# Folding a block-diagonal feature map into projection weights: one product of 128 rows, or two of 64 rows into two PSUM banks

## The chip, the cores and the metric

The kernel runs on one core of a Trainium2 chip. The metric is the device time of one execution in microseconds. A core has a matrix engine (PE in the profile, with its weight loads shown apart as PEld), a vector engine (DVE), a scalar engine (ACT), a general engine (POOL) and queues that issue DMA transfers (SP). PE writes its products to PSUM, which has eight banks; DVE and ACT read them from there.

## The reference, cut to what matters

Two models of width 1024 with 32 heads of 32 run on their own inputs of 2048 rows, and their outputs are put side by side. The first (A) is an attention with a compressed memory. The second (B) is a linear attention whose queries and keys pass through a learned map, one 32x32 matrix for each head, before two softmaxes:

```python
qkv = (x @ wqkv).reshape(B, S, 3, H, Dh).transpose(2, 0, 3, 1, 4)
q, k, v = qkv[0], qkv[1], qkv[2]
pq = einsum("bhsd,hdf->bhsf", q, w_phi)
pk = einsum("bhsd,hdf->bhsf", k, w_phi)
phi_q = concatenate([softmax(pq), softmax(-pq)], -1)
phi_k = concatenate([softmax(pk), softmax(-pk)], -1)
kv = einsum("bhsf,bhsd->bhfd", phi_k, v);  z = einsum("bhsf->bhf", phi_k)
o = einsum("bhqf,bhfd->bhqd", phi_q, kv) / (einsum("bhqf,bhf->bhq", phi_q, z)[..., None] + 1e-6)
return o.transpose(0, 2, 1, 3).reshape(B, S, D) @ wo
```

As (x @ w) @ phi = x @ (w @ phi), the kernel multiplies the weights of q and k by the map once and never computes q and k themselves.

## The kernel before, in words

**Stages.** From the start to about 900 us the attention of model A runs, in 32 units (`units`): a unit is one segment of 512 rows and one group of four heads. `produce` computes the projections of a unit, `values` its values, `attend` its scores, softmax, products with the values, and memory. Model B's keys and values follow, then its queries and output, then A's output projection. Large products are made of f16 halves (three products for each fp32 one) and partly by a Strassen scheme of seven products for eight.

**The fold.** Model B's weights are prepared while A runs. `fold(n, ...)` is called once for each unit, from `attend(u)` for unit u + 1, between the memory part and the scores, and once at the start; 32 calls in all. Four calls make one `quad`: 128 feature columns at two places of the output and two halves of the 1024 input columns. A call loads a tile `st` [128, 512] of transposed weights: 128 rows are the features of one group of four heads, 512 columns are inputs of the model. `phib` [128, 8, 128] holds the map; for each group its 128x128 block is zero but for four 32x32 blocks on the diagonal, one for each head. For each of four chunks of 128 columns, `st`'s chunk is the stationary operand (loaded as weights of the array) and `phib`'s block is streamed, all in fp32, into one PSUM bank [128, 4, 128] (line 1006). DVE then reads the bank, scales it by the factor `si` and writes a quarter of the quad in SBUF (line 1009). When a quad is whole, POOL forms sums and differences of its quarters (line 458), ACT and POOL split them into f16 halves (lines 465 and 466), and DMAs put them into the scratch tensor `wf_d`. Model B reads these forms much later. A call also loads the next quad's piece and measures its size (`size`, lines 980 to 994).

**The order of the work.** No engine's order is written by hand. Every operation is entered with `op(engine, dur, fn, r=..., w=..., prio=...)`: the microseconds that the planner books for it, what it reads and writes, and a priority. `Graph.run` then plays a list scheduler over those durations: it takes the engine that can start first and, on it, the startable operation with the lowest priority number, and emits the instructions in that order. The order is fixed before the kernel runs; on the chip the engines wait for each other by semaphores. `attend(u)` has priority 2u + 1, `fold` for the next unit 2u, `produce(u + 1)` 2u + 2.

**PSUM.** `bank(kind, shape, line)` asks the planner for one of the eight banks, and it is given at the first operation that uses it and comes free after the last. Kinds have a minimum that is kept for them and a maximum:

```python
KEEP = {"proj": 1, "s": 1, "misc": 1, "pv": 1, "kv": 0}
MOST = {"proj": 3, "s": 3, "misc": 2, "pv": 1, "kv": 4}
```

The fold uses a bank of the kind `misc`, and so do the row maxima (line 793), the memory's products (820), the transposed keys and the memory's update (835, 840), the transposed output (933), and the small products for scales and bounds (370, 657, 678). An operation that needs a bank starts when one can be given to its kind. Operations with the same `line` name open their banks in the order in which they were entered.

Of the kernel before, what the change touches and what calls it, by code (L numbers as in the profile page):

```python
# [13 lines left out]
OP = mybir.AluOpType  # L14
# [52 lines left out]
class Graph:  # L67
# [35 lines left out]
    def op(self, eng, dur, fn, r=(), w=(), prio=0, lat=0.0, short=False, port=False, need=(), kb=256):  # L103
        o = Op()
        o.short, o.port = short, port or eng == "POOL"
        o.eng, o.dur, o.fn, o.prio, o.lat, o.kb = eng, dur, fn, (prio, len(self.ops)), lat, kb
        o.banks = []
        ends, starts = set(), set()
        for b in need:
            if b.prev[0] is not None:  # L110
                ends.update(b.prev[0].ops)
        for write, accs in ((0, r), (1, w)):
            for acc in accs:
                b, key = acc if isinstance(acc, tuple) else (acc, None)
                old, last, opened = b.prev
                if old is not None:
                    ends.update(old.ops)
                if not b.ops and last is not None:
                    starts.add(last.ops[0])
                if opened is not None:  # L120
                    starts.add(opened)
                for k in (list(b.writer) if key is None else [key, None]):
                    if k in b.writer:
                        ends.add(b.writer[k])
                if write:
                    for k in (list(b.readers) if key is None else [key, None]):
                        ends.update(b.readers.pop(k, ()))
                    if key is None:
                        b.writer.clear()
                    b.writer[key] = o  # L130
                else:
                    b.readers.setdefault(key, []).append(o)
                b.ops.append(o)
                if b.kind is not None and b not in o.banks:
                    o.banks.append(b)
                    b.left += 1
        ends.discard(o)
        o.deps = [(d, 0) for d in ends] + [(d, 1) for d in starts - ends if d is not o]
        self.ops.append(o)
        return o  # L140
# [99 lines left out]
SP, PE, ACT, DVE, POOL = "SP", "PE", "ACT", "DVE", "POOL"  # L240
# [3 lines left out]
def tile_kernel(ctx: ExitStack, tc: tile.TileContext, ax, aw, awv, awo, beta, bx, bwqk, bwv, bphi, bwo, out):  # L244
    nc = tc.nc
# [68 lines left out]
    for t in vfb:  # L314
# [3 lines left out]
    op = G.op  # L318
# [5 lines left out]
       w=[gates], prio=0.2, lat=2.0, kb=16)  # L324
# [14 lines left out]
    def bank(tag, shape, line=None):  # L339
        b = G.bank(tag, shape, F32, line or tag)  # L340
        psums.add(b)
        return b
# [246 lines left out]
    for t in stk:  # L589
        op(ACT, 2.0, lambda t=t: nc.scalar.activation(t()[96:104, 1], sel[96:104, :, None].to_broadcast([8, 4, 512]), AF.Copy),  # L590
           w=[(t, (1, 3))], prio=0.3)
# [146 lines left out]
    def attend(u):  # L738
# [108 lines left out]
        if u + 1 < NU:  # L847
            fold(u + 1, 2 * u + 0)
# [92 lines left out]
    phib = G.buf("a", [128, NG, 128], F32, "phib")  # L941
# [25 lines left out]
    def fold(n, prio, dep=()):  # L967


        m, i = divmod(n, 4)  # L970
        which, gp, q, hb = 1 - m // 4, m % 4, i % 2, i // 2
        g = gp + 4 * hb

        def load(m, i):
            st = G.buf("stage", [128, 512], F32, "st", 2)
            op(SP, 0.6, lambda: nc.sync.dma_start(st(), bwqk[1 - m // 4, m % 4 + 4 * (i // 2), :, 512 * (i % 2):512 * (i % 2) + 512]),
               r=dep, w=[st], prio=prio, lat=1.0)
            return st

        def size(m, i):  # L980
            if i == 0:
                sizes[m] = (G.buf("a", [128, 4], F32, "twf", 1), G.buf("a", [128, 2], F32, "sif", 2))
            tw, si = sizes[m]
            st = load(m, i)
            op(ACT, 0.55, lambda: nc.scalar.activation(st(), st(), AF.Abs, accum_out=tw()[:, i:i + 1]), w=[st, (tw, i)], prio=prio)
            if i % 2:
                h = i // 2
                op(DVE, 0.1, lambda: nc.vector.scalar_tensor_tensor(
                    tw()[:, h:h + 1], tw()[:, 2 * h:2 * h + 1], tw()[:, i:i + 1], phs[:, m % 4 + 4 * h:m % 4 + 4 * h + 1],
                    op0=OP.max, op1=OP.mult), r=[(phss, m % 4 + 4 * h)], w=[tw], prio=prio)  # L990
            if i == 3:
                scale((tw, lambda: tw()[:, 0:2]), 2, (si, None, si), prio, top=13)
                op(DVE, 0.06, lambda: nc.vector.tensor_copy(swf[:, 1 - m // 4, m % 4:m % 4 + 1], si()[:, 0:1]),
                   r=[si], w=[(swfs, (1 - m // 4, m % 4))], prio=prio)

        if n == 0:
            for j in range(4):
                size(0, j)
        si = sizes[m][1]
        if i == 0:  # L1000
            quads[m] = G.buf("a", [128, 4, 512], F32, "quad", 1)
        qd = quads[m]
        st = load(m, i)
        ps = bank("misc", [128, 4, 128], "fold")
        for c in range(4):
            op(PE, 0.22, lambda c=c: nc.tensor.matmul(ps()[:, c, :], st()[:, c * 128:(c + 1) * 128], phib()[:, g, :],
                                                      start=True, stop=True), r=[st, phib], w=[ps], prio=prio, need=[qd])
        k = 2 * q + hb
        op(DVE, 0.62, lambda: nc.vector.tensor_scalar(qd()[:, k], ps().rearrange("p c n -> p (c n)"), si()[:, 1:2], None, op0=OP.mult),
           r=[ps, si], w=[(qd, k)], prio=prio)  # L1010
        if m < 7:
            size(m + 1, i)
        if i == 3:
            quads["prio"] = prio + 3
            forms(WPLAN, lambda k: (qd, k, lambda: qd()[:, k]),
                  out_halves(which, ("fo", "oT"), lambda d: d.rearrange("p a c n -> p (a c) n")[:, :, 128 * gp:128 * gp + 128]),
                  None, prio + 3, POOL)
# [44 lines left out]
    for f in (lambda: bounds(0, [1], 2.5), lambda: bounds(1, [1], 2.5), lambda: bounds_v(0, [1], 2.5)):  # L1062
        f()
    fold(0, 1, late)
    for u in range(NU):
        k = u // 2
# [65 lines left out]
    def pairv(t):  # L1132

        return t().rearrange("p (h a g d) -> p h a g d", h=2, a=2, g=8)
# [77 lines left out]
    for p in range(NT // 2):  # L1212
# [17 lines left out]
        for i in range(2):  # L1230
            if p in VT:
                n = 2 * VT.index(p) + i
                for hb in range(2):
                    op(SP, 0.6, lambda n=n, hb=hb, t=vs[i]: nc.sync.dma_start(
                        t()[:, 1056 * hb:1056 * hb + 1056], v_d[n, :, 1056 * hb:1056 * hb + 1056]), r=[(vdb, (n, hb))],
                       w=[(vs[i], (a, hb)) for a in range(2)] + [(vs[i], 2)], prio=P - 0.5, lat=1.5, kb=256)
# [8 lines left out]
        for hb in range(2):  # L1245
            for j in range(2):
                kv = bank("kv", [128, 4, 66], "sums")
                for i in range(2):
                    pt = G.buf("b", [128, 4, 4, 128], F16, "pt", 3)

                    def flat(e=es[i, hb], j=j):
# [3 lines left out]
                       r=[es[i, hb]], w=[(pt, 0)], prio=P)  # L1255
                    sub, ns, d = ((DVE, nc.vector, 0.6) if i else (POOL, nc.gpsimd, 1.28))
                    op(sub, d, lambda pt=pt, flat=flat, ns=ns: ns.tensor_tensor(pt()[:, 1], flat(), pt()[:, 0], op=OP.subtract),
                       r=[es[i, hb], (pt, 0)], w=[(pt, 1)], prio=P, port=True)

                    def f(i=i, j=j, hb=hb, kv=kv, t=vs[i], pt=pt):  # L1260
                        for k in range(4):
                            for a, b in ((0, 0), (0, 1), (1, 0)):
                                n = 64 if b else 65
                                nc.tensor.matmul(kv()[:, k, 0:n], pt()[:, a, k, :], pairv(t)[:, hb, b, 4 * j + k, 0:n],
                                                 start=(i == 0 and k == 0 and a + b == 0), stop=(i == 1 and a == 1), skip_group_check=True)
# [3 lines left out]
                def add(o, i, s, p=p):  # L1269
# [7 lines left out]
                   r=[kv, (pstb, (p, 0))], w=[(kva[hb], j)], prio=P)  # L1277
# [6 lines left out]
    for q in range(4):  # L1284
        ps = bank("misc", [128, 512])
        for i in range(4):
            op(PE, 0.22, lambda i=i, q=q, ps=ps: nc.tensor.matmul(
                ps()[:, 128 * i:128 * i + 128], za()[:, 4 * q + i:4 * q + i + 1].to_broadcast([128, 128]), ident,
                start=True, stop=True), r=[(za, (q // 2, q % 2))], w=[ps], prio=P)
# [3 lines left out]
       r=[(bigs, 1)], w=[(oscs, 1)], prio=P - 5)  # L1293
    op(DVE, 0.12, lambda: nc.vector.reciprocal(osc2[:, 1, 1:2], osc2[:, 1, 0:1]), w=[(oscs, 1)], prio=P - 5)
    kls = [G.buf("stage", [128, 2, 8, 64], F16, "st", 2) for _ in range(2)]
    for hb in range(2):
        zr, zs, v = G.buf("b", [128, 8], F32, "zr", 2), G.buf("b", [128, 8, 2], F32, "zs", 2), slice(8 * hb, 8 * hb + 8)
        op(DVE, 0.1, lambda zr=zr, v=v: nc.vector.tensor_scalar(zr(), za()[:, v], 1e-12, None, op0=OP.max),
           r=[(za, (hb, 0)), (za, (hb, 1))], w=[zr], prio=P)
        op(DVE, 0.12, lambda zr=zr: nc.vector.reciprocal(zr(), zr()), w=[zr], prio=P)  # L1300
        op(DVE, 0.1, lambda zr=zr: nc.vector.tensor_scalar(zr(), zr(), osc2[:, 1, 1:2], 2.0, op0=OP.mult, op1=OP.mult),
           r=[(oscs, 1)], w=[zr], prio=P)
        op(DVE, 0.1, lambda zr=zr, zs=zs: nc.vector.tensor_tensor(
            zs(), zr()[:, :, None].to_broadcast([128, 8, 2]), bm2[:, None, :].to_broadcast([128, 8, 2]), op=OP.mult),
           r=[zr], w=[zs], prio=P)
# [4 lines left out]
           r=[kva[hb]], w=[(kls[hb], 0)], prio=P)  # L1310
        op(DVE, 0.62, lambda hb=hb, v=v: nc.vector.tensor_tensor(kls[hb]()[:, 1], kva[hb](), kls[hb]()[:, 0], op=OP.subtract),
           r=[kva[hb], (kls[hb], 0)], w=[(kls[hb], 1)], prio=P, port=True)
    op(DVE, 0.1, lambda: nc.vector.tensor_scalar(osc2[:, 0, 0:1], big[:, 0:1], 4.0, None, op0=OP.mult),
       r=[(bigs, 0)], w=[(oscs, 0)], prio=P)
# [4 lines left out]
       r=[(wscs, (1, 0)), (wscs, (1, 1)), (oscs, 1)], w=[wo2b], prio=P)  # L1319
# [15 lines left out]
    for n in range(2):  # L1335
        for q in range(2):
            op(SP, 0.6, lambda n=n, q=q: nc.sync.dma_start(bo[n][q](), bo_d[n, q]), r=[(bob, (n, q))],
               w=[(bo[n][q], (a, i)) for a in range(2) for i in range(4)], prio=P + 1, lat=1.0, kb=1024)
# [44 lines left out]
    for c in range(NT):  # L1383
# [15 lines left out]
        if c == 14:  # L1399
            for i, f in enumerate(SECOND):  # L1400
                wform[f] = G.buf("slot", [128, 2, 4, 512], F16, f"S{i}")
                op(SP, 0.6, lambda i=i, f=f: nc.sync.dma_start(wform[f](), wo_d[i]), r=[(wob, i)],
                   w=[(wform[f], (a, n)) for a in range(2) for n in range(4)], prio=P + 0.5, lat=1.0, kb=1024)
# [5 lines left out]
        for hb in range(2):  # L1409
            e, r = er[c % 2, hb]  # L1410
            dn = G.buf("b", [128, 16, 2], F32, "dn", 2)
            for a in range(2):
# [3 lines left out]
                   r=[zb, r], w=[(e, ("x", a))], prio=P)  # L1416
# [10 lines left out]
               r=[e, r], w=[e], prio=P)  # L1427
            def flat(e=e):
# [4 lines left out]
               r=[e], w=[(eh, (hb, 0))], prio=P)  # L1433
            op(DVE, 1.13, lambda eh=eh, hb=hb, flat=flat: nc.vector.tensor_tensor(
                eh()[:, hb, 1], flat(), eh()[:, hb, 0], op=OP.subtract), r=[e, (eh, (hb, 0))], w=[(eh, (hb, 1))], prio=P, port=True)
            for a in range(2):
                op(SP, 0.6, lambda a=a, eh=eh, hb=hb, pt=pt: nc.sync.dma_start_transpose(pt()[:, a], eh()[:, hb, a]),
                   r=[(eh, (hb, a))], w=[(pt, a)], prio=P, lat=2.0, kb=256)
            pn = bank("pv", [128, 4, 128])

            def f(pn=pn, pt=pt, hb=hb):
# [11 lines left out]
               r=[pn, (ot, (0, hb))], w=[(ot, (1, hb))], prio=P)  # L1453
# [6 lines left out]
    for c in range(NT // 2):  # L1460
        P += 1
        A0, A1 = (G.buf("b", [128, 2, 4, 128], F32, "e", 5) for _ in range(2))
        for t, k in ((A0, c), (A1, c + 8)):
            op(SP, 0.6, lambda t=t, k=k: nc.sync.dma_start(t().rearrange("p h g t -> p (h g) t"), oa_d[k]),
               r=[osc], w=[t], prio=P, lat=1.0, kb=512)
# [105 lines left out]
```

## Time and profile before

| | |
|---|---|
| median of 3 runs | 1761.08 us (1757.87 to 1761.38) |
| profiled execution | 1762.63 us, span 1760.8 us |
| PE busy | 1692.6 us, 96% |
| DVE busy | 1404.1 us, 80% |
| ACT busy | 1129.7 us, 64% |
| POOL busy | 968.4 us, 55% |
| fold's products (line 1006) | 256 records, first at 62.3 us, last at 843.6 us |
| fold's DVE reads (line 1009) | 32 of 744 ns |

The span is the time from the first to the last instruction of one profiled execution. A record of PE lasts from its start until its result is out, so records of products overlap, and the pace of PE is read from start to start. PEld is the loading of weights, which overlaps the products before it. In a group's row stand the line, engine, operation, tiles and shapes, the count, and then busy microseconds, mean nanoseconds of one, and the idle time of the engine just before, with what ended it. In a timeline's row stand the start in microseconds, the time to the end of the last of the merged instructions, and their count.

### The profile page before, as it was taken

What the parts mean: (1) busy time and instruction counts of PE and PEld (TensorE: products, weight loads), DVE (VectorE), ACT (ScalarE), POOL (GpSimd) and SP (SyncE); (2) the same over time, 40 slices, a digit from 0 to 9 for tenths busy, and PEclk for the clock granted to TensorE, in tenths of its full rate; (3) what the DMA queues carried; (4) which work ended last, traced back from release to release, by engine and by line L of the source; (5) the groups of instructions that cost most, each with busy time, mean ns of one, the idle gap of its engine ahead of it and who ended that gap; (6) DMA issues with size and microseconds to landing.
All of it is one profiled execution on the core that took longest, in us unless ns stands there. A gap on an engine that the chain in (4) does not pass through costs nothing.

```text
span 1760.8 us, 38488 instructions
## 1 busy us (share of the span) xinstructions
PE 1692.6 (96%) x14456; PEld 1013.5 (58%) x14456; DVE 1404.1 (80%) x3207; ACT 1129.7 (64%) x2063; POOL 968.4 (55%) x1301
## 2 busy tenths in 40 slices
PE   8999999999999999999989999999899999989999
PEld 5767666667776766766744444444444444444444
DVE  5989989899777888788875998996988777677541
ACT  6887886978776787777774656554665544444431
POOL 6445454555757577866773535553578989650000
PEclk8999999999999999999999999999999999999999
DMA  5546546475445444567456343346646666665311
GB/s 191 183 147 178 143 144 182 150 219 170 145 137 152 119 134 122 152 197 184 129 183 254 114 140 137 138 146 236 225 138 168 156 164 147 141 187 159 120 66 66
DMA packets 240842, 275.67 MB, mean 157 GB/s; under 512 B 137488, under 2 KB 190480, under 8 KB 231952
## 3 DMA queue, kind: packets, MB, share of 16 engines
q1 hardware_dynamic: 240656, 273.22, 51.0%
q8 instruction: 113, 1.85, 0.4%
q14 instruction: 73, 0.60, 0.1%
HBM read 145.44 MB, written 85.00 MB: 131 GB/s over the span
## 4 chain that ended last, share of the span: by engine, by line
PE 58%; DVE 19%; ACT 5%; POOL 3%; issue 2%; DMA 1%; SPq 0%; ACTq 0%; DVEq 0%
PE proj L359 19%; PE proj L549 9%; PE proj L1499 5%; PE misc L359 5%; PE s L865 3%; PE pv L901 3%; PE s L767 2%; PE s L1499 2%; DVE s L773 2%; PE s L549 2%; DVE mx L1110 2%; DVE S L388 2%; DVE r L1120 1%; POOL e L1414 1%; PE misc L1499 1%
## 5 line engine op out<-in xcount | busy, mean ns | idle before, releaser
L359 PE MATMUL proj<-S,S 128*128 128x128 f16 (+1 forms) x3072 | 504.0, 300 | 5.2 <-ACT S L386 3.3
L359 PEld LDWEIGHTS <-S 128*128 128x128 f16 x4608 | 331.8, 99 | 154.8 <-issue 10.7
L549 PE MATMUL proj<-S,S 128*128 128x512 f16 x1488 | 351.0, 384 | 17.9 <-ACT cs L555 5.7
L549 PEld LDWEIGHTS <-S 128*128 128x128 f16 x1968 | 189.0, 99 | 237.9 <-issue 19.6
L878 POOL TENSOR_SCALAR_AFFINE_SELECT ph<-ph 128x256 f16<-128x256 f16 (+1 forms) x448 | 196.2, 459 | 178.8 <-DVE ph L872 142.7
L872 DVE SCALAR_TENSOR_TENSOR ph<-s,ph 128x512 f16<-128x512 f32 x320 | 210.5, 682 | 62.1 <-ACT ph L871 60.1
L773 DVE CUSTOM_DVE_ANT_0 s<-s,causal 128x512 f32<-128x512 f32 (+3 forms) x512 | 242.1, 509 | 12.2 <-PE s L767 8.7
L869 ACT ACTIVATE s<-s,bd 128x512 f32<-128x512 f32 x320 | 212.7, 712 | 24.5 <-PE s L865 24.1
L871 ACT ACTIVATE ph<-s 128x512 f16<-128x512 f32 x320 | 190.8, 657 | 1.2 <-PE pv L901 0.5
L359 PE MATMUL misc<-S,ot 128*128 128x512 f16 x768 | 171.7, 381 | 1.5 <-ACT ot L1449 0.9
L1117 ACT ACTIVATE e<-e,sk 128x256 f32<-128x256 f32 x256 | 114.8, 498 | 77.9 <-DVE e L1114 76.7
L359 PEld LDWEIGHTS <-ot 128*128 128x128 f16 x768 | 73.8, 98 | 91.5 <-DVE ot L1451 2.0
L767 PE MATMUL s<-S 96*128 96x512 f16 (+3 forms) x512 | 113.3, 300 | 6.0 <-DVE mt L773 4.2
L865 PE MATMUL s<-S 104*128 104x512 f16 (+3 forms) x512 | 114.4, 302 | 1.9 <-ACT S L795 0.8
L1414 POOL TENSOR_TENSOR e<-e,zb 128x512 f32<-128x512 f32 x64 | 81.6, 1284 | 50.3 <-DVE r L1120 49.7
L359 PE MATMUL proj<-wv,S 128*128 128x128 f16 x1536 | 104.3, 221 | 0.3 <-DVE mt L773 0.3
L901 PEld LDWEIGHTS <-ph 128*128 128x128 f16 x2560 | 87.8, 96 | 19.0 <-POOL ph L878 2.4
L901 PE MATMUL pv<-vl,ph 128*128 128x66 f16 (+1 forms) x2560 | 93.0, 185 | 2.5 <-POOL ph L878 1.6
L1120 DVE TENSOR_REDUCE r<-e 128x32 f32<-128x1024 f32 x64 | 76.8, 1204 | 10.1 <-ACT e L1117 9.8
L549 PE MATMUL s<-S,S 128*128 128x512 f16 x324 | 76.3, 379 | 0.0
L719 ACT ACTIVATE h<-proj,bd 128x512 f16<-128x512 f32 x64 | 47.6, 748 | 44.0 <-PE proj L359 43.8
L773 DVE DVE_READ_ACCUMULATOR2_ANT mt<- 128x1 f32 x512 | 71.9, 140 | 0.0
(313 smaller groups left out, 3268.9 us busy)
## 6 DMA issues: line engine op xcount, KB each, us to landing
S<-h SPq DMA_DIRECT2D x192, 128.0 KB
S<-wf_d SPq DMA_DIRECT2D x21, 1024.0 KB
st<-bwqk SPq DMA_DIRECT2D x64, 256.0 KB
wf_d<-fo SPq DMA_DIRECT2D x48, 256.0 KB
out<-os SPq DMA_DIRECT2D x40, 256.0 KB
wf_d<-oT SPq DMA_DIRECT2D x36, 256.0 KB
S<-xf_d SPq DMA_DIRECT2D x9, 1024.0 KB
S<-aw SPq DMA_DIRECT2D x16, 512.0 KB
```

The costliest lines, as they stand in the source:

```text
L359: op(PE, dur, lambda c=c, a=a, b=b, lv=lv, rv=rv: nc.tensor.matmul(pv(), lv(), rv(), start=(c == 0 and a + b == 0), stop=(c == n - 1 and a ...
L549: op(PE, 0.215, lambda n=n, a=a, b=b, lv=lv, rv=rv: nc.tensor.matmul(ps(), lv(), rv(), start=(start and n == 0 and a + b == 0), stop=(n == ...
L767: nc.tensor.matmul(ps()[:, o:o + 128 * i + 128], st()[0:96, 0, h, 128 * i:128 * i + 128], st()[0:96, 1, h, 0:128 * i + 128], start=True, s ...
L773: dve(0.12 + 0.00113 * n, lambda h=h, i=i, o=o, n=n: nc.vector.tensor_tensor_reduce(ps()[:, o:o + n], ps()[:, o:o + n], causal[:, 512 - n: ...
L865: nc.tensor.matmul(ps()[:, o:o + n], st()[0:104, 1, h, 128 * j:128 * j + 128], st()[0:104, 0, h, 128 * j:512], start=True, stop=True)
L869: act(0.59, lambda: nc.scalar.activation(ps(), ps(), AF.Exp, bias=0.0, scale=bd()[:, 4, i2, 0:1]), r=[(bd, i2)], w=[ps])
L871: act(0.5, lambda: nc.scalar.activation(ph()[:, 0], ps(), AF.Copy, scale=2.0 ** 14), r=[ps], w=[(ph, 0)])
L872: dve(0.6, lambda: nc.vector.scalar_tensor_tensor(ph()[:, 1], ps(), 2.0 ** 14, ph()[:, 0], op0=OP.mult, op1=OP.subtract), r=[ps, (ph, 0)], ...
L878: nc.gpsimd.affine_select(pd, pd, pattern=[[0, n], [1, 128]], compare_op=OP.is_ge, fill=0.0, base=0, channel_multiplier=-1)
L901: nc.tensor.matmul(ps()[:, i, n0:n1], ph()[:, a, o:o + 128], vl()[:, j, h, n0:n1], start=(i == 0 and a == 0), stop=(j == min(i, 2)), skip_ ...
L1117: op(ACT, 0.41, lambda i=i: nc.scalar.activation(e()[:, 4 * i:4 * i + 4], e()[:, 4 * i:4 * i + 4], AF.Exp, bias=0.0, scale=sk()[:, i:i + 1 ...
L1499: op(PE, 0.215, lambda n=n, a=a, b=b: nc.tensor.matmul(ps(), v(a)[:, n, :], wform[w]()[:, b, n, :], start=(start and n == 0 and a + b == 0 ...
```

## The change

Each of the four products of a fold (128 rows, 128 streamed columns) becomes two: rows 0 to 63 of `st` with the upper left 64x64 block of the map, and rows 64 to 127 with the lower right one. The first kind goes into one misc bank, the second into another; each bank holds [128, 4, 64]. The stationary operand of each is 64 rows by 128 columns, the streamed one 64 rows by 64 columns. The first product is an operation of its own, which opens the first bank; the other seven are one operation, which opens the second. The planner books 0.06 and 0.4 us for them, where it booked four times 0.22. DVE reads the two banks with one instruction each (booked at 0.36, before one at 0.62), and each writes 64 of every 128 columns of the quarter.

```diff
-        ps = bank("misc", [128, 4, 128], "fold")
-        for c in range(4):
-            op(PE, 0.22, lambda c=c: nc.tensor.matmul(ps()[:, c, :], st()[:, c * 128:(c + 1) * 128], phib()[:, g, :],
-                                                      start=True, stop=True), r=[st, phib], w=[ps], prio=prio, need=[qd])
         k = 2 * q + hb
-        op(DVE, 0.62, lambda: nc.vector.tensor_scalar(qd()[:, k], ps().rearrange("p c n -> p (c n)"), si()[:, 1:2], None, op0=OP.mult),
-           r=[ps, si], w=[(qd, k)], prio=prio)
+        ps = [bank("misc", [128, 4, 64], "fold") for _ in range(2)]
+
+        def f(*some):
+            for c, a in some:
+                v = slice(64 * a, 64 * a + 64)
+                nc.tensor.matmul(ps[a]()[:, c, :], st()[v, c * 128:(c + 1) * 128], phib()[v, g, v], start=True, stop=True)
+
+        op(PE, 0.06, lambda: f((0, 0)), r=[st, phib], w=[ps[0]], prio=prio, need=[qd])
+        op(PE, 0.4, lambda: f((0, 1), *((c, a) for c in range(1, 4) for a in range(2))), r=[st, phib], w=ps, prio=prio, need=[qd])
+        for a in range(2):
+            op(DVE, 0.36, lambda a=a: nc.vector.tensor_scalar(
+                qd()[:, k].rearrange("p (c n) -> p c n", n=128)[:, :, 64 * a:64 * a + 64], ps[a](), si()[:, 1:2], None, op0=OP.mult),
+               r=[ps[a], si], w=[(qd, k)], prio=prio)
```

## The prediction

> **What bounds the kernel now.** I read the page first, then the chain of waits from 60 to 850 us (the stretch that holds all 32 folds), then groups and timelines around the changed lines.
>
> ```profile
> span 1760.8 us, 38488 instructions
> PE 1692.6 (96%) x14456; PEld 1013.5 (58%) x14456; DVE 1404.1 (80%) x3207; ACT 1129.7 (64%) x2063; POOL 968.4 (55%) x1301
> PE 58%; DVE 19%; ACT 5%; POOL 3%; issue 2%; DMA 1%; SPq 0%; ACTq 0%; DVEq 0%
> ```
> ```profile
> by line: PE proj L359 40.9%; PE s L865 5.9%; PE pv L901 5.7%; PE s L767 4.9%; DVE s L773 4.7%; DVE ph L872 2.0%; PE misc L1006 1.9%; PE misc L820 1.8%; PE misc L840 1.5%; DVE S L388 1.3%; PE misc L933 1.2%; issue 1.1%; ACT s L869 1.1%; ACT
> ```
> ```profile
> core 0: us, PE busy (x) PEld busy (x) DVE busy (x) ACT busy (x) POOL busy (x), PEclk, DMA share, GB/s
> 100.00:200.00 100.00, 98.98 (x1086) 71.07 (x1084) 89.56 (x238) 82.03 (x150) 51.50 (x81) 1.00 0.54 165
> 500.00:600.00 100.00, 100.00 (x1059) 69.95 (x1057) 80.65 (x254) 67.70 (x123) 62.22 (x89) 1.00 0.45 128
> ```
> PE ends most waits. In the stretch of the folds it is busy 99 to 100 of every 100 us, and the PE lines that the chain names add up to 64% of it. The granted clock there is 1.00. The fold's products (L1006) hold 1.9% of the chain's 790 us, 15 us. So PE time given or taken here counts, though not all of it.
>
> **The fold before.** Groups from 60 to 850 us (busy, mean ns of one), then the timeline of one fold.
>
> ```profile
> L359 PEld LDWEIGHTS <-S 128*128 128x128 f16 x4188 | 300.8, 99 | 133.4 <-issue 4.1
> L767 PEld LDWEIGHTS <-S 96*128 96x128 f16 x462 | 42.2, 98 | 35.2 <-issue 9.3
> L1006 PE MATMUL misc<-phib,st 128*128 128x128 f32 x256 | 36.1, 279 | 0.1
> L1006 PEld LDWEIGHTS misc<-phib,st 128*128 128x128 f32 x256 | 33.3, 191 | 3.2 <-PE s L865 0.4 <-DVE mh L788 0.3 <-DVE mt L773 0.2
> L1009 DVE TENSOR_SCALAR quad<-misc,sif 128x512 f32<-128x512 f32 x32 | 23.8, 744 | 4.4 <-PE misc L1006 4.1 <-POOL ph L878 0.2
> L827 DVE TENSOR_TENSOR amem<-misc,dm 128x256 f32<-128x256 f32 x42 | 17.6, 420 | 0.8
> ```
> ```profile
> 62.26 0.38 PE L359 MATMUL proj<-S,S 128*128 128x512 f16 x1
> 62.26 1.07 PEld L1006 LDWEIGHTS misc<-phib,st 128*128 128x128 f32 x8
> 62.47 1.05 PE L1006 MATMUL misc<-phib,st 128*128 128x128 f32 x8
> 63.36 0.59 PE L359 MATMUL proj<-S,S 128*128 128x512 f16 x2
> ```
> Each fp32 product is two passes: 256 records for 32 folds of four products. From the first pass to the next line's product is 63.36 - 62.47 = 0.89 us; (1.05 - 0.28) / 7 = 0.110 us for each pass. The first weight load starts at 62.26, under the product before it. All folds: 32 x 0.89 = 28.5 us of PE time.
>
> **What sets those 0.110 us?** This decides the case, since the change halves what each product streams (64 columns of the map in place of 128) but loads 128 weight columns as before, twice as often. The timeline has fp32 products that stream one or two columns:
>
> ```profile
> 715.44 0.34 PE L657 MATMUL misc<-wgb,xam 128*128 128x2 f32 x2
> 715.64 0.58 PE L678 MATMUL misc<-wvb,xam 128*128 128x1 f32 x4
> 716.08 0.36 PE L657 MATMUL misc<-wgb,xam 128*128 128x2 f32 x2
> ```
> Four passes of L678, one column each, fill 715.64 to 716.08: 0.110 us a pass, as with 128 columns. So the fp32 weight load alone is a floor of 0.110 us, and a narrower stream saves nothing above it. Nor do fewer rows shorten a load where the trace shows it: 96 rows take 98 ns, 128 rows 99 ns (L767, L359, f16). Loads of 64 fp32 rows aren't in the trace.
>
> The Trainium skill (TensorE: Matmul & The Clock Gate, LDWEIGHTS) says the same against this change: load time goes by columns, not rows, at columns / 1.2 GHz, which for 128 is an estimated 107 ns. By that rule the trace's 0.110 stands for 64 rows too.
>
> **Two tiles side by side, and the switch.** The trace has a relative: L1445, products with 64 weight columns that go in pairs to two halves of the array. (The second fence is from the fold phase, for the pace of 512-column products.)
>
> ```profile
> 1309.19 1.03 PE L359 MATMUL misc<-S,ot 128*128 128x512 f16 x4
> 1310.15 0.86 PE L1445 MATMUL pv<-pt,st 128*64 128x128 f16 x24
> 1310.94 0.60 PE L359 MATMUL misc<-S,ot 128*128 128x512 f16 x2
> ```
> ```profile
> 155.81 1.24 PE L359 MATMUL proj<-S,S 128*128 128x512 f16 x5
> ```
> The 24 take 0.79 us to the next line, 0.033 each, 0.066 a pair, where L359's 128-column weights stream 512 columns in (1.24 - 0.38) / 4 = 0.215, thus 128 in about 0.055. One after the other they would need 24 x 0.055 = 1.32. Pairs do overlap. But the ends cost: the product before starts last at 1309.19 + 1.03 - 0.38 = 1309.84 and has streamed at 1310.055, and the pairs begin 0.095 later. The last pair starts at 1310.15 + 0.86 - 0.22 = 1310.79, has streamed at 1310.845, and the next product comes 0.095 later. I take 0.095 for going into the split array and for coming out. This split is by columns, the change's by rows; below, the cost is 0 if a split by rows needs no emptying.
>
> **The new fold, step by step.** Sixteen passes, in order two of the upper half, two of the lower, and so on. Passes of unlike halves overlap, those of one half can't, so the loads run as one alone, seven pairs, one alone: nine steps of 0.110 = 0.99. Plus 0.095 in, 0.055 for the last stream (128 columns of f16; 64 of fp32 at the rate of at most 0.110 for 128), 0.095 out: 1.235 us, against 0.89. That is +0.345 a fold, 11.0 us over 32. Without the two switches it would be 1.045, +0.155 and 5 us; the rivals hold the ends farther out.
>
> **The two banks.** The first product now opens one misc bank alone and the other seven wait for a second; at most two misc banks exist, and the matrices of memory, keys, rows, output and bounds use them as well.
>
> ```profile
> 414.15 0.61 PE L1006 MATMUL misc<-phib,st 128*128 128x128 f32 x4
> 414.59 0.38 PE L865 MATMUL s<-S 104*128 104x384 f16 x2
> 414.81 0.66 PE L1006 MATMUL misc<-phib,st 128*128 128x128 f32 x4
> 415.31 0.62 PE L820 MATMUL misc<-mem,pq 128*128 128x132 f32 x4
> 417.22 0.74 DVE L1009 TENSOR_SCALAR quad<-misc,sif 128x512 f32<-128x512 f32 x1
> ```
> Here a fold holds its bank from 414.15 to 417.96, 3.8 us, while L820 has the other. Where the other is held, the planner puts full-array products between the two parts of the fold, as it put L865 between these. Each such break costs another 0.19 for out and in, 0.11 for one more unpaired step, 0.055 for a stream: 0.355. Between no fold and all 32 (11.4 us) I take half, since some six tenants with holds of one to three us share the other bank in about 26 us of a unit (my estimate from this hold): 16 x 0.355 = 5.7. The tenants that now wait until both banks are read cost between 0 and about 16 x 1 us; I take 0, because PE has ready L359 products to fill in, and keep the rest for the range. Without that cover the scores would stand behind the late rows.
>
> **DVE, DMA, POOL.** One read of 512 (0.744) becomes two of 256. The nearest row is L827, 256 from PSUM in 0.420: 0.84, +0.096, 3.1 us over 32. L1009 isn't among the chain's named lines, so I count a fifth, 0.6; bounds 0 and 3.1. Loads of the weights (two DMAs a fold) and POOL's combinations behind it are as before; POOL has cover:
>
> ```profile
> POOL quad L458 <- DVE quad L1009: 27.8, 6, 19.5
> ```
> It waited 27.8 us for the quads in six waits and is busy half to two thirds of the stretch; if that cover were gone, each later quad would delay wf_d, first read hundreds of us later.
>
> **Sum.** PE 11.0 + 5.7 = 16.7 us. How much of it reaches the end: the chain holds 15 of the 28.5 us of today's folds, 0.53; with PE busy 99%, at most 1. I take 0.7: 11.7, plus 0.6 for DVE: +12.3. The planner's books (0.46 for a fold, 0.88 before) move the order a little either way; I price that at 0 and give it 5 us in the range. The profiled execution took 1762.63 us for its span of 1760.8; the median of the runs shown is 1761.08, 1.55 below it. The sum against the profiled execution gives 1774.9, and at the runs' level 1773.
>
> **Rivals.**
> 1. The halves don't overlap: fp32 loads of one half wait for the other, or single halves run as full-array products with a switch each time. Sixteen passes x 0.110 + 0.245 = 2.0, +1.11 a fold, with breaks 41 us; by 0.7 to 1, +29 to +41: 1790 to 1802. For it: the order goes by twos of one half, unlike L1445's alternation. Against it: those pairs overlap fully. 12%.
> 2. Faster, by one mechanism: loads of 64 fp32 rows pass in half the time (0.055) and a split by rows empties nothing. Nine steps of 0.055 + 0.055 = 0.55, -0.34 a fold, -10.9, by 0.7 -7.6: 1753.5. It decides from a step under about 0.07 with free switches; with 0.095 at each end and the breaks it comes out near nothing. Against it: L678's floor and the equal loads at 96 and 128 rows. 16%.
> 3. No change: fold time on PE grows, but falls into time in which PE would have waited for DVE (busy 81 to 90%) and ACT; the pass-through is then under 0.2, +3 or less: 1761 to 1764. For it: DVE and others hold a third of the chain. Against it: PE at 99%. 14%.
>
> The Trainium skill (TensorEngine Tiling (Array Packing), Theoretical Speedup) promises up to two times for contractions of at most 64 rows; taken at its word a fold would take 0.89 / 2 = 0.445 and the kernel about 10 us less, 1751, which is rival 2's direction. The same page (Key Properties) says that a change of tiling mode drains the engine, which the 0.095 at both ends of L1445 agrees with.
>
> **Numbers.** Forecast 58%: 1773, own range 1765 to 1785. Faster than 0.2% (about what a measurement of this kernel can tell) is rival 2, 0.16; same is rival 3, 0.14; slower 0.70. The range reaches from 1757, between no change and rival 2, to 1797, inside rival 1.
>
> **What would show it.** Right: 512 product records of the fold with 64 rows, loads near 190 ns as now, about 1.2 us from a fold's first pass to the next line where unbroken, a gap of some 0.1 us before and after; DVE 64 reads of 0.40 to 0.45; the fold's share of the chain up by half. Wrong: a fold in under 0.8 us, or no gap at its ends (rival 2); 1.8 or more (rival 1); fold as priced but the span within 3 us (rival 3).

## The result and the profile after

The changed kernel takes 1784.65 us (median of 4 runs, 1784.34 to 1788.62); the kernel before, 1759.8 in the same series. The ratio is 1.0147, 95% interval 1.0134 to 1.0159: about 26 us slower by the ratio, 24.9 by the medians. The forecast was 1773, with a range to 1797.

The page of the changed kernel, then its chain of waits from 60 to 870 us, which holds the folds:

```profile
span 1786.8 us, 39033 instructions
PE 1714.6 (96%) x14712; PEld 1022.9 (57%) x14712; DVE 1422.7 (80%) x3239; ACT 1133.2 (63%) x2063; POOL 967.0 (54%) x1301
PE 63%; DVE 20%; ACT 6%; POOL 6%; DMA 3%; issue 3%; SPq 0%; ACTq 0%; DVEq 0%; POOLq 0%
```
```profile
by line: PE proj L359 45.9%; PE s L865 6.4%; PE pv L901 6.2%; PE s L767 6.0%; PE misc L1010 4.9%; DVE s L773 4.3%; PE misc L820 2.2%; PE misc L840 2.1%; DVE ph L872 2.1%; ACT ph L871 1.8%; ACT s L869 1.8%; issue 1.7%; DVE S L388 1.6%; PE mi
```
The fold's products (now L1010) hold 4.9% of the chain's 810 us, 40 us, where they held 15.

Groups from 60 to 870 us, and the timeline of PE around a fold in one piece and one in two:

```profile
L1010 PE MATMUL misc<-phib,st 64*128 64x64 f32 x512 | 45.4, 284 | 2.0 <-DVE ph L872 0.8 <-ACT vf L705 0.7 <-DVE mt L773 0.4
L1010 PEld LDWEIGHTS misc<-phib,st 64*128 64x128 f32 x512 | 38.1, 191 | 15.7 <-issue 4.1 <-DVE ph L872 2.2 <-DVE mt L773 1.8
L1015 DVE TENSOR_SCALAR quad<-misc,sif 128x256 f32<-128x256 f32 x62 | 28.9, 475 | 19.4 <-PE misc L1010 19.4
```
```profile
91.98 0.59 PE L359 MATMUL proj<-S,S 128*128 128x512 f16 x2
92.50 1.11 PE L1010 MATMUL misc<-phib,st 64*128 64x64 f32 x16
93.55 0.61 PE L359 MATMUL proj<-S,S 128*128 128x512 f16 x2
```
```profile
161.67 0.60 PE L359 MATMUL proj<-S,S 128*128 128x512 f16 x5
162.20 0.43 PE L1010 MATMUL misc<-phib,st 64*128 64x64 f32 x2
162.57 0.23 PE L359 MATMUL proj<-S,S 128*128 128x128 f16 x1
162.73 1.10 PE L1010 MATMUL misc<-phib,st 64*128 64x64 f32 x14
163.76 0.34 PE L359 MATMUL proj<-S,S 128*128 128x128 f16 x3
```
The 16 passes take 1.04 us to the next line's product (1.041 before the rows are rounded). The product before them starts last at 91.98 + 0.59 - 0.38 = 92.19 and has streamed 0.215 later, at 92.405; the fold begins 0.09 after that. So a fold in one piece takes 1.13 us of PE for 0.89. In two pieces it takes 0.37 + 1.03 and twice the 0.09, 1.58. Of the 32 folds, 21 run in two pieces (counted over the records of L1010). That makes 11 x 1.13 + 21 x 1.58 = 45.6 us of PE for 28.5, 17.1 more. The 28.5 are 32 times the one fold of 0.89; counted over all folds in the records, to the next product each time, the changed kernel comes to 45.7 and the kernel before to 29.7, since some of its folds take up to 1.04: 16.0 more. A read on DVE takes 0.475 us, two of them 0.95 for 0.744.

### The profile page after: what moved, and what is told of

Its sections match the earlier page's. It is cut to its first block, busy times and chain, and to the rows that moved or that the text cites. A ratio compares the mean times of both kernels' runs of the same rounds, so it can differ in the third digit from the quotient of the medians.

```text
span 1786.8 us, 39033 instructions
## 1 busy us (share of the span) xinstructions
PE 1714.6 (96%) x14712; PEld 1022.9 (57%) x14712; DVE 1422.7 (80%) x3239; ACT 1133.2 (63%) x2063; POOL 967.0 (54%) x1301
## 4 chain that ended last, share of the span: by engine, by line
PE 63%; DVE 20%; ACT 6%; POOL 6%; DMA 3%; issue 3%; SPq 0%; ACTq 0%; DVEq 0%; POOLq 0%
PE proj L359 24%; PE proj L549 8%; PE proj L1506 5%; PE misc L359 4%; PE s L865 3%; PE s L767 3%; PE pv L901 3%; PE s L1506 2%; DVE s L773 2%; PE misc L1010 2%; DVE mx L1117 2%; DVE S L388 2%; POOL e L1421 2%; PE s L549 2%; DVE r L1127 2%
## 5 line engine op out<-in xcount | busy, mean ns | idle before, releaser
L359 PE MATMUL proj<-S,S 128*128 128x128 f16 (+1 forms) x3072 | 512.1, 301 | 4.3 <-ACT S L386 3.6
L359 PEld LDWEIGHTS <-S 128*128 128x128 f16 x4608 | 329.4, 99 | 151.4 <-issue 10.4
L773 DVE CUSTOM_DVE_ANT_0 s<-s,causal 128x256 f32<-128x256 f32 (+3 forms) x512 | 242.8, 510 | 13.4 <-PE s L767 9.5
L871 ACT ACTIVATE ph<-s 128x512 f16<-128x512 f32 x320 | 186.4, 638 | 0.9 <-PE pv L901 0.2
```

What stands on the lines that cost most here:

```text
L359: op(PE, dur, lambda c=c, a=a, b=b, lv=lv, rv=rv: nc.tensor.matmul(pv(), lv(), rv(), start=(c == 0 and a + b == 0), stop=(c == n - 1 and a ...
L773: dve(0.12 + 0.00113 * n, lambda h=h, i=i, o=o, n=n: nc.vector.tensor_tensor_reduce(ps()[:, o:o + n], ps()[:, o:o + n], causal[:, 512 - n: ...
L871: act(0.5, lambda: nc.scalar.activation(ph()[:, 0], ps(), AF.Copy, scale=2.0 ** 14), r=[ps], w=[(ph, 0)])
```

## The experiments

Where two kernels ran in different series, I compare their ratios to the kernel before, and turn them into us with its 1759. By the intervals of the ratios, such a difference is good to 3 to 5 us either way.

**1. The changed order with the old products.** The planner's entries are untouched, so every engine does the same things in the same order; what the two PE operations issue is another, and the two reads write other columns of the quarter (not among the lines below; a read takes 472 ns for 475).

```diff
-                v = slice(64 * a, 64 * a + 64)
-                nc.tensor.matmul(ps[a]()[:, c, :], st()[v, c * 128:(c + 1) * 128], phib()[v, g, v], ...)
+                nc.tensor.matmul(ps[c // 2]()[:, c % 2, :], st()[:, c * 128:(c + 1) * 128], phib()[:, g, :], ...)
```

> Same order of the work on every engine, same banks and same two DVE reads as the changed kernel, but the products are the old ones of 128 rows: two of the four chunks go into one bank, two into the other. Nothing of the computation is left out. In the changed kernel a fold in one piece takes 1.04 us from its first pass and 0.09 before it, a fold in two pieces 0.36 + 1.03 and twice 0.09; 11 and 21 of them make 45.6 us against 28.5 before, so 17 us of PE time. Theory A (the 64-row products' PE time is the loss): PE gets the 17 us back, the kernel comes to about 1785 - 17 = 1768, and 8 us stay with the order, the held banks and DVE. Theory B (the order and the two held banks are the loss, and PE time only fills waits): the kernel stays within 6 us of the changed one, 1779 or more.

Measured 1770.42 us, ratio 1.0059 (1.0043 to 1.0075). The 64-row products cost 1.0147 - 1.0059, 15.5 us. The 17 us that were expected take 28.5 for the old products; in this order these are broken 21 times too and take 30.4 by all records, so the PE time between the two kernels is 45.7 - 30.4 = 15.3 us: theory A holds. Another 10.4 us stay without them.

**2. No fold in two pieces.** The planner's `bank` and `start` are taught to ask for two banks at once, and the eight products are one operation booked at 0.46.

```diff
-        op(PE, 0.06, lambda: f((0, 0)), r=[st, phib], w=[ps[0]], ...)
-        op(PE, 0.4, lambda: f((0, 1), *((c, a) for c in range(1, 4) for a in range(2))), r=[st, phib], w=ps, ...)
+        op(PE, 0.46, lambda: f(*((c, a) for c in range(4) for a in range(2))), r=[st, phib], w=ps, ...)
```

> The eight 64-row products are one operation that starts only when two misc banks are free, so no fold is cut in two. Theory A: 21 folds lose their second way in and out, 1.59 - 1.13 = 0.45 us each, 9.5 us together: about 1775. Theory B: a fold now waits for two free banks and the order is another again; the gain is under 4 us or there is a loss.

Measured 1759.08 us, ratio 0.9998 (0.9981 to 1.0015): 26 us faster than the changed kernel, where the breaks explain 21 x 0.45 = 9.5. Neither theory allowed for that. The order is another from 62 us on, and experiment 8 will show what it is worth.

**3. The kernel before with light books.** Not one instruction is another, only the planner's price.

```diff
-            op(PE, 0.22, lambda c=c: nc.tensor.matmul(ps()[:, c, :], ...
+            op(PE, 0.115, lambda c=c: nc.tensor.matmul(ps()[:, c, :], ...
```

> The kernel before, with its four products booked at 0.115 us each in the planner, 0.46 a fold, as the changed kernel books them; the instructions are the same and only the order is another. If the order that follows from the light books is part of the loss, this is 4 us or more above the kernel before, 1764 or more; if not, within 3.5 us of it, 1756 to 1763. Theory A says the second, theory B the first.

Measured 1771.27 us, ratio 1.006 (1.0042 to 1.0079): 10.6 us slower by the ratio, 12.5 by the medians. Theory A said this would cost nothing, and that was wrong. Where it is lost, slices of the kernel before (first fence) and of this one (second) show; columns are the busy time of PE, PEld, DVE, ACT and POOL, then granted clock, DMA share and rate, and the last row sums eight slices from 840 to 1000 us:

```profile
900.00:920.00 20.00, 17.26 (x150) 9.79 (x147) 16.63 (x47) 13.22 (x24) 16.80 (x20) 0.99 0.52 154
920.00:940.00 20.00, 16.34 (x122) 7.76 (x123) 10.70 (x17) 12.89 (x24) 13.74 (x21) 0.74 0.74 256
940.00:960.00 20.00, 20.00 (x97) 9.34 (x95) 12.23 (x19) 4.97 (x9) 4.37 (x8) 1.00 0.85 322
sum 160.00, PE 149.24 PEld 84.54 DVE 123.42 ACT 104.25 POOL 95.55; mean PE 18.65 PEld 10.57 DVE 15.43 ACT 13.03 POOL 11.94
```
```profile
900.00:920.00 20.00, 10.39 (x54) 5.39 (x54) 12.50 (x38) 10.91 (x19) 8.77 (x12) 0.70 0.48 129
940.00:960.00 20.00, 16.52 (x64) 6.71 (x65) 7.86 (x11) 9.30 (x15) 8.39 (x10) 0.83 0.33 131
sum 160.00, PE 136.59 PEld 74.68 DVE 113.15 ACT 87.58 POOL 88.63; mean PE 17.07 PEld 9.34 DVE 14.14 ACT 10.95 POOL 11.08
```
The last fold starts at 845 us, before at 844, and attention's last sums (line 924) start at 930, before at 943: nothing is lost among the folds. The first sums of model B's keys (line 1120) come at 979, before at 967. The loss lies between, where attention runs out and model B begins: PE is busy 12.7 us less in these 160, and the granted clock falls to 0.70. The kernel before has such a dip too, but in one slice (0.74 from 920 to 940). Experiment 1 has no such hole: its PE is busy 147.9 us from 840 to 1000, its first sums of the keys come at 971, and half of its loss lies behind them. Why this order begins model B late is not shown.

**4. Quadrants.** Each 64-row product of the changed kernel is cut into two of 64 weight columns, in the changed order.

```diff
-                nc.tensor.matmul(ps[a]()[:, c, :], st()[v, c * 128:(c + 1) * 128], phib()[v, g, v], ...)
+                for m0 in (0, 64):
+                    nc.tensor.matmul(ps[a]()[m0:m0 + 64, c, :], st()[v, c * 128 + m0:c * 128 + m0 + 64], phib()[v, g, v], ...)
```

> The changed kernel with each 64-row product cut in two of 64 weight columns, which go to the two column halves of the array: 32 passes a fold, four at a time. If the load of 128 weight columns sets the step of 0.112 us (theory A), the step falls to about 0.056 and a fold in one piece from 1.04 to about 0.65 us from its first pass; with 32 folds some 11 us less, about 1774. If the step is set by issue or by the switch of the array, a fold stays at 1.0 us or more and the time at 1782 or more.

Measured 1771.23 us, ratio 1.0072 (1.0047 to 1.0096), 13.2 us under the changed kernel where theory A said 11. The timeline of the same fold, and the loads' group from 60 to 870 us:

```profile
90.15 0.59 PE L359 MATMUL proj<-S,S 128*128 128x512 f16 x2
90.67 0.69 PE L1011 MATMUL misc<-phib,st 64*64 64x64 f32 x32
91.30 0.61 PE L359 MATMUL proj<-S,S 128*128 128x512 f16 x2
```
```profile
L1011 PEld LDWEIGHTS misc<-phib,st 64*64 64x64 f32 x1024 | 22.0, 136 | 15.7 <-DVE ph L872 3.2 <-issue 3.2 <-ACT vf L705 1.7
```
Twice the passes, the same columns streamed by each, the same rows, half the weight columns in each load: the fold falls from 1.04 to 0.63 us. The seven steps from the first group of passes to the eighth, on average (1.11 - 0.27) / 7 = 0.12 us in the changed kernel, are (0.69 - 0.23) / 7 = 0.066 here. (By the records' own starts the first step is the longest, and the others are 0.112 and 0.058.) The load's columns set the step; they are also the rows that a product writes, and no run separates the two, but the kernel before already had 0.110 with one streamed column. The Trainium skill (TensorE: Matmul & The Clock Gate, LDWEIGHTS) has load time go by columns and not by rows; the trace agrees with both halves of it: 64 rows saved nothing, 64 columns half.

**5. Unbroken, with true books.** As experiment 2, booked at what the trace of the changed kernel showed.

```diff
-        op(PE, 0.46, lambda: f(...
+        op(PE, 1.13, lambda: f(...
-            op(DVE, 0.36, lambda a=a: ...
+            op(DVE, 0.475, lambda a=a: ...
```

> The unbroken 64-row fold with the planner's books at what the trace of the changed kernel shows: 1.13 us for the products with the way in, 0.475 for each read. Theory A (PE time of the fold counts, the order is luck within some 10 us either way): within 10 us of the unbroken kernel with light books, 1750 to 1770, and no steady gain. Theory C (light books make bad orders, since the planner lets others start too early): at least 4 us faster than with light books, 1755 or less.

Measured 1737.53 us, ratio 0.9887 (0.9871 to 0.9902): 20 us faster than the kernel before, with the dearer products and reads. This fits theory C and lies outside theory A's 10 us.

**6. Unbroken quadrants,** booked at 0.72 and 0.475, the edits of experiments 2 and 4 together.

> Unbroken, with quadrants of 64 by 64, booked at 0.72 and 0.475 as their trace has it. A fold should take 0.63 us from its first pass and 0.09 before, 0.72 against 0.89 in the kernel before, -5.4 us of PE time over 32; DVE reads 0.95 against 0.74, +6.6 us of DVE time. Theory A: 1748 to 1762, by the order; a real gain over the kernel before shows only if PE counts more than DVE. If DVE counts as much as PE: 1757 or more.

Measured 1755.49 us, ratio 0.998 (0.997 to 0.999): 3.5 us faster than the kernel before. It is slower than experiment 5, although its fold is 0.41 us shorter; the order differs.

**7. The kernel before with repeated products.** Same order, 12 passes a fold for 8.

```diff
-            op(PE, 0.22, lambda c=c: nc.tensor.matmul(ps()[:, c, :], ..., start=True, stop=True), ...
+            op(PE, 0.22, lambda c=c: [nc.tensor.matmul(ps()[:, c, :], ..., start=True, stop=True) for _ in range(2 if c % 2 else 1)], ...
```

> The kernel before in its own order, with two of a fold's four products issued twice into the same place: 12 passes for 8, +0.44 us a fold, 14.2 us of PE time over 32, and nothing else is another. This measures how much of PE time in the fold reaches the end. The prediction took 0.7 (bounds 0.53 and 1): +7.5 to +14.2 us, about 1769. If PE time only fills waits: under +4.

Measured 1766.69 us, ratio 1.0049 (1.0034 to 1.0064): 8.6 us (6 to 11 by the interval) of 14.2, 0.6 of the added PE time reaches the end.

**8. The order of experiment 2 with the old products.**

```diff
-            for c, a in some:
+            for c in some:
-                nc.tensor.matmul(ps[a]()[:, c, :], st()[v, c * 128:(c + 1) * 128], phib()[v, g, v], ...)
+                nc.tensor.matmul(ps[c // 2]()[:, c % 2, :], st()[:, c * 128:(c + 1) * 128], phib()[:, g, :], ...)
```

> The order of the unbroken 64-row kernel, instruction for instruction, with the old products of 128 rows over the two banks. A fold goes from 1.04 + 0.09 to about 0.89, 0.24 us each, 7.8 us over 32. Theory A: 5 to 8 us faster than the unbroken 64-row kernel, 1751 to 1754, and thus faster than the kernel before by an order that is better by luck. Theory B: no difference over 2 us.

Measured 1749.92 us, ratio 0.9954 (0.9939 to 0.997): 7.7 us faster than experiment 2 by the ratios, for 6.9 us of PE time (36.2 and 29.3 by all records). It also has two reads and two held banks for each fold and is still faster than the kernel before; what these cost by themselves can't be told apart from the order. Its instructions are those of experiment 1, with the same banks and reads, and it is 18.5 us faster (1.0059 - 0.9954): that is the order alone, and about what the breaks left unexplained in experiment 2 (26 - 9.5).

**9 and 10. The kernel before with other books,** 0.27 and 0.17 in the place of 0.22.

> The kernel before with the fold's products booked at 0.27 each, 1.08 a fold, for 0.88; same instructions, another order. Booked at 0.46 it was 12.5 us slower than at 0.88. Theory C (heavier books make better orders): 1755 or less. Theory A (the order is luck within some 10 us): anywhere from 1748 to 1772.

> The same, booked at 0.17 each, 0.68 a fold. Theory C: between the kernel before and that booked at 0.46, 1760 to 1770. Theory A: anywhere from 1748 to 1772, and not in the order of the books.

Measured 1746.5 us, ratio 0.9928 (0.9908 to 0.9948), and 1750.32, ratio 0.995 (0.9932 to 0.9968). The first is what theory C said, and just below the range of theory A; the second contradicts theory C: 0.17 is lighter than 0.22 and yet 8.8 us faster.

**11. The order of experiment 5 with the old products** (the edit of experiment 8).

> The order of the 64-row unbroken kernel that is booked at 1.13 us, instruction for instruction, with the old products of 128 rows over the two banks. A fold takes 0.89 us of PE for 1.13: 0.24 x 32 = 7.8 us of PE time. At the share that the repeated passes showed (7.9 us of 14.2, 0.55) to all of it: 4 to 8 us faster than the 64-row one's 1737.5, 1730 to 1733. If it is no faster, the 64-row products cost nothing in a good order.

Measured 1733.5 us, ratio 0.9855 (0.984 to 0.987): the fastest of all, 25 us under the kernel before, and 5.6 us under experiment 5 for 7.4 us of PE time (36.3 and 28.9). Its page, and what the stretch of 60 to 850 us holds in it (second fence) and in the kernel before (third):

```profile
span 1731.8 us, 38529 instructions
PE 1677.4 (97%) x14456; PEld 1010.1 (58%) x14456; DVE 1404.2 (81%) x3239; ACT 1131.0 (65%) x2063; POOL 967.5 (56%) x1301
```
```profile
60.00:850.00 790.00, 785.42 (x8600) 561.52 (x8598) 696.10 (x2025) 636.57 (x1155) 489.52 (x765) 1.00 0.53 158
```
```profile
60.00:850.00 790.00, 777.73 (x8486) 554.91 (x8483) 677.75 (x1936) 624.87 (x1135) 479.76 (x751) 1.00 0.53 155
```
It gets 114 more products done in the same 790 us, and 89 more DVE instructions, of which up to 32 are there because a fold has two reads for one: work packed closer on all engines. Its last fold starts at 823 us, before at 844, and the first sums of model B's keys come at 941.5, before at 967.3: 26 of the 29 us between the two profiled spans are won by there.

**12. The same unbroken old products, booked at 0.89.**

> The unbroken fold of 128-row products over two banks, booked at what it takes, 0.89, and 0.475 for each read; at 0.46 it was 1749.9. Theory C (books near or above the true price make better orders): 1745 or less, between 1750 and the time of the one booked at 1.13. Theory A (luck): anywhere from 1730 to 1765.

Measured 1747.42 us, ratio 0.9927 (0.9906 to 0.9947). It lies between its neighbours (0.46: 1749.92; 1.13: 1733.5), though above the 1745 that theory C named.

**Taken together.** One kind of work, several orders:

| work of a fold | booked at (us): time (us) |
|---|---|
| four products of 128 rows, one bank | 0.46: 1771.3; 0.68: 1750.3; 0.88 (before): 1759; 1.08: 1746.5 |
| the same into two banks, in two pieces 21 times (experiment 1) | 0.46: 1770.4 |
| the same into two banks, unbroken | 0.46: 1749.9; 0.89: 1747.4; 1.13: 1733.5 |
| eight products of 64 rows, unbroken | 0.46: 1759.1; 1.13: 1737.5 |

Along the first row the instructions are the same and the time moves by 24.8 us, not in the order of the books. The second and third row also share their instructions, and differ by up to 36.9 us. In each row with several books the heaviest is the fastest, but three rows are no rule (and where a fold is unbroken, the reads are booked at 0.36 beside 0.46 and at 0.475 beside the others): theory C stays open. What is shown is that the order of the same instructions moves this kernel by some 25 to 37 us in all. What makes an order good is not shown.

The PE time in the next table is counted over all folds of both traces, from the first pass of a piece to the next product, with 0.09 for each way into the split; the few pieces after which PE waits are taken at the median.

| same order, unlike products | PE time (us) | whole time by the ratios (us) |
|---|---|---|
| changed kernel against experiment 1 | 15.3 | 15.5 |
| changed kernel against experiment 4 | 15.3 | 13.2 |
| experiment 2 against 8 | 6.9 | 7.7 |
| experiment 5 against 11 | 7.4 | 5.6 |
| experiment 7 against the kernel before | 14.3 | 8.6 |

## Why the prediction was right or wrong

The direction and the range held, and the likeliest case was the right one; the size was half of what came (+12.3 forecast, +25 measured). Two things in that were luck. The forecast's own range ended at 1785, 0.35 us above the measurement, and reached on to 1797 only for rival 1, which fell. And the direction hung on an order that the prediction didn't look at: unbroken and in the orders of experiments 2 and 5, the same 64-row products come out level with the kernel before and 20 us faster. What was no luck is that the products cost PE time and that this time reaches the end.

- **The floor of the weight load** held. Loads of 64 rows kept 191 ns a record, as predicted, and the half stream saved nothing. Experiment 4 shows the cause by halving the columns.
- **Overlap of the halves** held, so rival 1 fell. All 16 passes go in pairs, so the nine steps became eight pairs, 0.84 us from the first pass's start to the last's for 0.99, and 1.13 us with the way in came out for 1.235. The way in was 0.09 for 0.095; the way out was dearer, 0.20 from the last pass's start for 0.055 + 0.095 = 0.15. A split by rows is emptied like the split by columns that the trace had, so rival 2 fell.
- **The breaks** were 21, taken as 16, and each cost 0.45 us for 0.355, as the lone first product takes 0.37 to the next line. Cheaper folds and more, dearer breaks nearly cancel, by luck: 17.1 us of PE time for 16.7. The 28.5 us of today's folds were read from one fold; all 32 take 29.7, which leaves 16.0.
- **How much of PE time reaches the end**: 0.7 was taken, between 0.53 and 1. In the changed order it was 15.5 us for 15.3, all of it; in the other pairs 0.6 to 1.1, and good to 3 to 5 us each. The term was some 4 us low here. The changed kernel's chain says the same: its folds hold 40 of their 45.7 us.
- **DVE**: the row of L827 (0.420) was a poor stand-in; the reads take 0.475, outside the 0.40 to 0.45 that was named, 6.6 us more DVE time over 32 for 3.1. The changed kernel's share of it can't be told apart from the order.
- **The step that failed** is "I price that at 0 and give it 5 us in the range", on the planner's books. Without the 64-row products the changed order is 10.4 us slower than the old (experiment 1). The same instructions in the order of experiment 8 are 18.5 us faster than that, so the loss belongs to the order and not to the two banks or the reads as such. The light books alone, without a second bank, cost the kernel before as much (10.6, experiment 3), so a loss of this size needs neither. It isn't the same loss, or not all of it: experiment 3 loses everything in the hole at the handover, which experiment 1 doesn't have, and experiment 1's last fold is 5 us late already, experiment 3's 1 us. What in the changed order costs the 10.4 us stays open.
- **Rival 3**, no change: PE time did not vanish into waits in any of the five pairs.

## What to carry to other kernels

Before halving the rows and the streamed columns of an fp32 product, ask what sets its pace: products in the trace that stream one column show the price of the weight load, and here that price, and not the stream, set the step. Where a planner fixes the order from booked durations, compare an edit in one and the same order (leave the books, swap the instructions), since orders of the same instructions lay 25 and 37 us apart here, where the products of this change cost 15.5. And such a planner is worth trying with other books: the old products in the order of experiment 11, though with two banks and two reads for each fold, made the kernel 1.45% faster.

## What the hardware showed that was not expected

Four fp32 products run side by side in quadrants of 64 by 64, with average steps of 0.066 us for 0.12 in halves of 64 rows: a fold with half the zeros left out is cheaper on PE (0.63 + 0.09) than the full product (0.89) only in this form, of those tried. Leaving the split costs more with halves than with quadrants: from the last pass's start to the next product's, 93.55 - (92.50 + 1.11 - 0.27) = 0.21 us, 0.20 by the records' own starts, against 0.15 by the same records in experiment 4; no run tells why. And where an order leaves PE idle, the granted clock falls as well: at the handover of experiment 3 it was 0.70 in a slice where PE was busy 10.4 of 20 us. It does not follow the busy share slice by slice (in the kernel before, 0.99 at 17.3 us and 0.74 at 16.3), and how much of the loss it makes is not shown.
